# A gated mix of attention and a long convolution on one Trainium2 core: the convolution's tail taken in two halves of the channels

## The chip, the cores and the metric

One core of a Trainium2 chip (trn2) runs the whole computation in one launch. The metric is the device time of one execution in microseconds (us); lower is better.

## What is computed

With `x` of 2048 tokens by 512 channels in bf16, the result is `g*a + (1-g)*b`, where `g` is a sigmoid gate for each token. Cut to what matters, the reference is:

```python
x = A_x
g = sigmoid((x * gate_w).sum(-1, keepdims=True))
# a: 32 heads of 16 channels, 4 segments of 512 tokens, taken in order
for s in range(4):
    p = softmax(causal(q_s @ k_s.T * scale))
    o_s = gh * (phi(q_s) @ M) / (phi(q_s) @ z) + (1 - gh) * (p @ v_s)
    M, z = M + phi(k_s).T @ v_s, z + phi(k_s).sum()
a = concat(o) @ wo
# b: for each channel a kernel K of 2048 lags made of 128 complex exponentials,
# a causal convolution of x with K by FFT, and a skip term
K = einsum('dn,dnl,dn->dl', C, exp(dt*A*l), dt*B).real
b = irfft(rfft(pad(x)) * rfft(pad(K)))[:2048] + x * Dskip
return g * a + (1 - g) * b
```

## The kernel before

The program is recorded as a graph of operations (helpers `op`, `dma` and `evac`, L176 to L247) and replayed in an order that is written out as the string `ORDER` (L372): a list of the numbers of the operations, with a letter for those evictions that may run on either VectorE (`v`, called DVE) or ScalarE (`a`, called ACT). Each engine runs its share of that list strictly in the list's sequence, and so does the one DMA queue, which belongs to SyncE (SP). An operation waits on semaphores for what it reads and for the buffers that it takes. Almost every PE instruction of the program carries the line L646, every eviction L240 to L244 and every transfer L236, since helpers record them.

The work falls into these parts.

- *Powers* (`ssm_powers`, L741): ten repeated squares of a complex exponential for the two halves of the channels, 20 tiles of 2 KB in each partition (pool `pw`). DVE copies and negates parts of each tile (L761, L763).
- *Attention* (`project`, `scores`, `seg_state`, `ophase`): 4 segments by 4 groups of 8 heads. A group has five score tiles. For each, PE writes scores to four of the eight PSUM banks, ACT takes the exponential of 128x2048 elements (L1021, 80 of them), and PE multiplies by the values (`pv`). All else shares the other four banks.
- *Tables* (`tables`, L1090): the kernel K is built for 128 channels at a time, c = 0 to 3. DVE makes two tables of powers, F (20 entries) and G (32 entries), by complex products in three instructions each (L1118, L1121, L1125), in a layout with two channels side by side (inner runs of 2 elements). PE then multiplies them with many small matmuls of 20 columns (`lag`), and four transfers put the result in `KTT`. There is one buffer for F and one for G.
- *First level of the transform* (`x_level1`, L800): 32 matmuls of 512 columns over `x`, evicted and written to a scratch in DRAM, `scr_Z`.
- *Tail of the convolution* (`tail`, L1173): 16 steps t over the frequencies, each for all 512 channels. Step t loads 256 KB of `scr_Z` (Zx) and 448 KB of constants (CT, the tensor `c_DN`). `X`: two matmuls with the matrix M2, two evictions, and two transfers that swap the tile's halves of partitions. `K`: for each of two frequencies, five matmuls of 512 columns over `KTT` and an eviction. `Y`: a product on DVE (L1220). `V`: two matmuls each and an eviction. One transfer then scatters 256 KB to 8 partitions of `V2`.
- *Final* (end of `tail`): for each of 16 row blocks, `fin` adds the attention's output projection and the skip term, `fir` adds two matmuls over `V2`, and a scaled eviction and a transfer write the result. Six of the `fin` may run before the last V.

The tail's buffers (pools of phase 2, from `a = T0`) lie over F, G, the powers and the tables' scratch. A tile of phase 2 waits until the tiles of phase 1 that lay there are done with, so no step of the tail can load before the last table is used.

Of the kernel before, what the change touches and what calls it, by code (L numbers as in the profile page):

```python
# [11 lines left out]
H = 32  # L12
# [100 lines left out]
class Sched:  # L113
# [120 lines left out]
    def dma(self, out, in_, nbytes, r=(), w=(), pw=(), key=None, slow=False, q="SP"):  # L234
        kw = {"allow_slow_non_contiguous": True} if slow else {}
        return self.op(q, ("D", nbytes), lambda e: e.dma_start(out(), in_(), **kw), r=r, w=w, pw=pw, key=key, isdma=True)  # L236

# [118 lines left out]
def c_pe(mode, *ns):  # L356
    return ("P", mode, ns)


LQ = "SP"  # L360
NPT = 5
GA, TA0 = 2.6, 10.0
TT0, TT = 8.0, 26.0
XL0, XLS = 20.0, 20.0
TK0, TDK = 120.0, 7.0
NOPEN = 6
PW, PWS = (1.0, 8.0), 0.6
# [5 lines left out]
192 53 0 204 8 394 9 14 12 13 54 10 56 11 55a 15 22 28 57v 16 3 26 23a 1 24 17 27v 25a 1234 29 30 202 376 32 31 33 4  # L373
34 252 203a 18 35 36 44 2 199 253a 37 39 20 38 40 249 19 41 200a 42 21 43 201 211 172 5 173 7 218 219 45 6 47 207 48
46 49 52 58 209 174 50 175 61a 51 220 67v 68 69 66 176 59 60 72 212v 70 239 62 64 63 240 71 188 82 84 65 205 85a 83 78
241 86 87 189 190 191 193 76 227 194 97a 228 77 210a 98 99 94 208v 195 229 73v 213 74 75 95 96 106 108 235 90 206a 236
107 109v 118 221 120 237 119 133v 134 135 110 111 121a 196 79v 222 130 80 122 223 123 88 131 132 91a 234 144 224 238
89 102 242 177 243 178 142 225 100 179 226 230 143 145a 157v 154 156 103a 158 155 159 197 101 250a 114 112 1240 146
115a 147 113 124 126 104 127a 105 125 136 138 116 214 117 137 139a 150 180 148 166a 149 160 162 181 163a 161 92 169a
93 198 128 1002a 170 1003a 171 1008 1004a 129 251 1005a 215 261 1006a 1007 1241a 1010 262 1011 151a 1012 182 1009 1242  # L380
263 1016 183 184 1235 185 186 187 1017 1018 1236a 1022 265 1243a 1023 266 1244 1024 1237 267 1013 295 1014 1015 216
164 165 1238a 81 140 270 141 296a 271 231 1239 232 233 217 272 1025 292 377 1026 293a 278 378a 279 1027 379 280 1255
264 268 1038 269 273 274 380a 282 275 276 283 294 244 245 254 246 284 1245 152 153 1019 247 1020 1021 1028 248a 306
1029 255 307 1246a 1030 256 1247 257 308 277 1034 281 258 1037 1248a 311 1249 259 312 260 1039 1250 313 1252 1035 336
1276 1036 1251a 302 1253a 303 333 337a 167 1254 168 304 1031 1266 1268 1032 285 286 287 288 334a 289 319 1033 1267a
320 290 321 305 1040 309 291v 310 314 1256 1041 1258 1042 1269a 323 1043 1257a 324 1044 1270 1259a 1045 297 318 335
325 322 315 1260 316 1046 317 1047 1048 1049 298 345 1050v 346 299 1051 347 300 1052 1053 1054 301 1060v 1061v 1062v
1063a 1064v 349 1055a 1068 350 1069 1056 1070 1261 1074 351 1263 1057 326 1075 327 1058 1076 1078 1059 328 329 330
1262a 354 1080 1264a 355 1081 331 1265 356 386 1082 348 1083 352 353 332a 362 1084 387a 363 389 364 1271 1085 357 390a
358 366 359 1272a 367 360 393 391 1273 388 1092 338 591 368 1277 392 1093 1274a 408 339 1094 1275 409 1278a 1279 410  # L390
397 340 341 1280v 1065 1281 1066 1067 412 398a 1071 413 1072 342 1073 414 399 1077 343 344 443 1079 1086 400a 361 1087
425 444a 426 365 1088 427 401 1089 395 1090 402a 1091 429 396a 430 445 1098 411 431 1099 446 1100 1101 1282 1102 369
370 1103 447a 415 609 371 417 1283a 372 450 418 373 448 1095 374 419 1284 381 416 449 382 375v 493 1096 1285a 462 383
384 1286 463 494a 385 424 495 420 464 1097 403 1292 428 432 421 433 422 434 404 435 458 436 1293a 459 423 1104 405 460
1105 406 1106 1107 1109 1108v 1110 475 476 1111 477 1112 461 1113v 407 1118v 1114 1124 1294 1119v 1120v 1121a 1287
1115 1122v 479 1295a 1126 480 1127 1116 1288a 1128 1289 1117 1132 481 465 1133 496 1296 1134 1297 1138 466 1139 1290a
467 497a 468 1291 1140 592 498 500 1141 594 469 806 499 1142 593a 523 524 1143 470 525 1298 1123 1125 1129 1299a 1130
515 1131 595a 516 471 472 473 1300 1135 517 1136 541 1137 1144 1145 1301a 451 1146 542a 1302 1303 452 1147 1305 1304a
1148 1306a 474 506 1149 1307 507 543 1308 453 508 478 454 1310 1156 455 1157 482 1158 483 456 1309a 527 484 1311a 485
528 486 457 1312 437 529 1150 544 1313 438 439 545a 440 510 1314a 511 548 1151 546 441 512 487 1315 547 442v 488 509  # L400
489 1316a 490 565 566 1317 1152 513 567 514 491 522 1153 526 501 530 492a 531 1154 556 502 557 601 558 532 533 534 518
1155 549 602a 560 1159 550 561 1160 604 1161 562 503 504 1162 603 551 1163 552 1164 519 520 605a 1165 521 573 1166a
608 574 606 1167 575 1168 607 1169 1170 505 1171v 553 1176v 1172 1177a 1182 1178a 623 1194 1173 1179a 554 624 1180a
535 1174 555 625 1184 559 1175 536 563 537 564 538 568 711 569 570 571 644 712a 1181 645 1183 713 715 539 1185 658
1186 646 714 1190 1191 610 1192 1196 596 540a 627 1197 659a 628 611a 1198 572 576 629 1187 616 1188 1189 612 1199 617a
577 613a 578 1200 614 579 1201 661 615a 1212 632 662a 633 626 634 1193 630 1195 631 807 1202 580 1203 581 824 808a 640
1204 641 660 635 1208 642 639 636 1211 690 691 1213 643 692 1209 647 648 1210 677 678 597 582 598 599 583 600 809 637
638 679 584 1205 618 666 1206 810a 673 1207 674 1214 675 708 1215 1216 1217 1218 619 1338 1219 694 667 709v 695 1357
620 1220 1358 696 621 668 1221 1319 669 1222 710 1223 1320 649 650 1225 651 1339 1226 1224a 1227 1228 738 1318 1229a
739 676 1230 740 680 1231 681 585 1232 622 586 587 1233 670 663 588 682 683 671 589 672 684 664 759 590v 665 756 760v  # L410
721 757a 722 652 758 723 689 693 763 653 697 654 698 655 685 761 686 775 687 776 688 699 1351 700 777 701 762 1332
1352v 780 1333a 781 724 782 1327 702 1328v 771 703 772 704 997 705 773 706 998 999 742 1000 707a 1001 743 774 744 716
816 778 817v 779 783 717 730 784 731 785 786 656 718 732 719 819 818 657v 720 820v 764 725 821 823 737 726 765 822 741
766 727 745 767 746 954 747 748 749 768 955v 837 769 728 838 729 770 733 800 734 735 825 736 801 802 788 839 826a 789
803 871 790 956 750 872v 831 875 873 751 752 792 832a 793 753 911 874 794 754 912v 862 755v 811 833 913 812 827 813
834 815 829 828v 787 814 830v 842 791 835 843 795 863 864 796 957 797 798 799 865 958a 804 854 844 959 905 805v 855
849 906 836 907 840 908 841 845 960 850 846 847 868 848 851 856 914 869v 1321 870 915a 1323 852 897 1322v 1395 1324a
1359 898 853 918 1325 1360v 1361 857 1326 1362v 858 1340 1342 1414 1341v 1343a 1363 1397 859 885 1398a 860 1364 1399
861 886 1344 1329 866 1345 1334 1330 1376 1370 867v 1331a 1433 887 1400a 1335 1371v 916 1401 1346 1336a 1353 1402 1372
1337 1354 1347a 1378 899 1377 1380 1355a 876 1566 1379v 1381a 1365 877 1348 1382 917 1383 1373 1366v 1349 1374v 1435  # L420
1453 1350a 1437 979 1367 1436a 1384 1356 1438v 980 1471 878 1439 1368 1385v 879 1440 1369v 1416 1418 1396 1417a 880
981 1389 1375 1386 1419a 1528 881 961 1420 1465 1390v 1421 1391 1387 1466a 882 893 1388a 1392 894 883 1415 1393v 884
888 1473 889 1475 1394 1474v 1403 1452 1476v 1408 895 1477 1404a 890 891 1478 1405 923 1409a 948 924 1410 1406 1460
1407v 949 950 1422 1461a 951 925 1411 1423a 1454 1472 1412v 1456 1455a 892 919 1490 1424 1457a 896 1413 920 1425 1458
900 1426v 901 1427 1459 902 903 904 928 921 1428a 909 929 1429 922 926 910v 1479 1467 1430 1480a 930 1468 1434 1431a
1492 1481 936 1469a 1432 1494 1493v 937 927 1484 1509 1495v 1462 1496 931 935 932 1497 1485a 1463 938 966 933 1491
1464a 1486 1441 967 934 1470 1487 1442v 1482 1488v 1511 1529 1483a 940 968 1513 1512a 1489 1530 941 1514v 939 1547
# [9 lines left out]
1629 1661 1642a 1643 1662 1659 1663a 1660v 1664  # L437
"""


def v2_row(t):
    return 64 * (t >> 3) + 32 * ((t >> 2) & 1) + (t & 3)

# [903 lines left out]
```

## Time and profile before

Three timed runs gave 379.22, 384.55 and 379.0 us; the median is 379.22. The profiled execution took 382.91 us, of which the span from the first to the last instruction is 381.1.

| | PE | DVE | ACT | DMA |
|---|---|---|---|---|
| busy, us | 298.8 | 275.0 | 275.1 | |
| share of the span | 78% | 72% | 72% | 31% of 16 engines |
| instructions or packets | 4268 matmuls | 627 | 322 | 25755, 36.07 MB |

Busy time is the time in which at least one instruction of the engine was under way. A matmul's end is modelled, so a busy PE need not be a PE at its best rate. The clock granted to PE was 0.87 of its full rate on the mean. The shares are averages over stages that differ much, so the stages are read one by one in the prediction.

### The profile page before, as it was taken

Reading aid. Unit: us, or ns where it says so; the run is one execution under the profiler, and the core shown is the slowest. Engines: PE = TensorE matmul, PEld = TensorE weight load, DVE = VectorE, ACT = ScalarE, POOL = GpSimd, SP = SyncE. Lnnn points to the kernel's source line nnn. Section 1 sums busy time; section 2 is a strip of 40 time slices with the busy share of each in tenths; the row PEclk is TensorE's granted clock in tenths of the full one; section 3 lists DMA queues with packets and bytes.
Section 4 is the critical chain, followed back from the end, with each engine's and each line's share of the span. In section 5 each row is a group of like instructions: output and inputs, shape, how many; then the busy total and the mean of one; then the engine's idle time right before and its main releaser. Section 6 shows DMA issues by size and latency. Waiting matters only on the chain.

```text
span 381.1 us, 9878 instructions
## 1 busy us (share of the span) xinstructions
PE 298.8 (78%) x4268; PEld 170.4 (45%) x4268; DVE 275.0 (72%) x627; ACT 275.1 (72%) x322; POOL 3.2 (1%) x9
## 2 busy tenths in 40 slices
PE   3856167877696768879955899999969888788994
PEld 3314024455353534556532657655323433334551
DVE  0699999996998499978996352989768687644011
ACT  4599999788995589797965485789947786544242
POOL 1000000000000000000000000000000000000000
PEclk9965559689997586999968696999989999999998
DMA  7900002121200061101005500002797587663113
GB/s 180 321 15 1 3 28 84 64 104 49 84 29 29 3 184 58 57 3 21 2 2 156 204 3 2 2 2 56 233 248 210 172 245 210 187 174 110 34 75 146
DMA packets 25755, 36.07 MB, mean 95 GB/s; under 512 B 9200, under 2 KB 13808, under 8 KB 25584
## 3 DMA queue, kind: packets, MB, share of 16 engines
q1 hardware_dynamic: 25712, 35.45, 31.0%
q8 instruction: 33, 0.54, 0.6%
q14 instruction: 10, 0.08, 0.1%
HBM read 20.10 MB, written 6.29 MB: 69 GB/s over the span
## 4 chain that ended last, share of the span: by engine, by line
DVE 40%; PE 34%; DMA 14%; ACT 5%; issue 5%; SPq 2%; ACTq 0%
PE psum L646 33%; DVE sb L1118 8%; DVE sb L1125 8%; DVE sb L1121 7%; DMA sb<-c_DN 5%; DMA sb<-sb 5%; DMA sb<-scr_Z 3%; DVE sb L241 3%; ACT sb L1021 2%; DVE sb L996 2%; SPq L236 2%; DVE sb L753 1%; DMA sb<-in_B_C_im_dram 1%; DVE sb L752 1%; DVE sb L763 1%
## 5 line engine op out<-in xcount | busy, mean ns | idle before, releaser
L646 PE MATMUL psum<-sb 128*128 128x17 bf16 (+12 forms) x4132 | 287.2, 239 | 68.9 <-ACT sb L1021 21.6
L646 PEld LDWEIGHTS psum<-sb 128*128 128x128 bf16 (+3 forms) x4132 | 159.9, 100 | 193.9 <-issue 46.8
L1021 ACT ACTIVATE sb<-psum 128x2048 bf16<-128x2048 f32 x80 | 150.3, 1879 | 26.9 <-PE psum L646 26.4
L240 ACT ACTIVATE sb<-psum 128x512 bf16<-128x512 f32 (+2 forms) x143 | 85.0, 623 | 49.5 <-PE psum L646 41.4
L241 DVE CAST sb<-psum 128x512 bf16<-128x512 f32 (+1 forms) x66 | 43.7, 675 | 34.1 <-PE psum L646 29.4
L1118 DVE TENSOR_TENSOR sb<-sb 128x512 bf16<-128x512 bf16 (+3 forms) x52 | 35.8, 690 | 0.8
L1125 DVE TENSOR_TENSOR sb<-sb 128x512 bf16<-128x512 bf16 (+3 forms) x52 | 34.7, 669 | 1.5
L1121 DVE TENSOR_TENSOR sb<-sb 128x512 bf16<-128x512 bf16 (+3 forms) x52 | 35.5, 685 | 0.1
L1220 DVE TENSOR_TENSOR sb<-sb 128x1024 bf16<-128x1024 bf16 x32 | 21.7, 687 | 7.7 <-ACT sb L240 4.7
L244 DVE TENSOR_SCALAR sb<-psum,sb 128x512 bf16<-128x512 f32 x5 | 3.8, 751 | 21.4 <-PE psum L646 21.4
L243 ACT ACTIVATE sb<-psum,sb 128x512 bf16<-128x512 f32 x11 | 7.6, 687 | 14.8 <-PE psum L646 14.8
L996 DVE TENSOR_TENSOR sb<-psum,sb 128x256 bf16<-128x256 f32 x32 | 13.4, 423 | 0.9
L1033 DVE TENSOR_TENSOR sb<-sb 128x1024 bf16<-128x1024 bf16 (+1 forms) x20 | 11.5, 573 | 0.0
L751 ACT ACTIVATE sb<-sb 128x512 f32<-128x512 f32 x18 | 11.0, 626 | 0.1
L684 PE MATMUL psum<-sb 128*128 128x128 bf16 x64 | 5.8, 254 | 6.1 <-DMA sb<-c_ident 4.7
L993 DVE RECIPROCAL sb<-psum 128x16 f32<-128x16 f32 x32 | 8.0, 250 | 1.2 <-PE psum L646 1.1
L943 DVE TENSOR_SCALAR sb<-sb 128x512 bf16<-128x512 bf16 x16 | 5.6, 349 | 4.4 <-ACT sb L240 4.4
L759 ACT ACTIVATE sb<-sb 128x512 bf16<-128x512 f32 x14 | 8.7, 620 | 0.0
L952 ACT ACTIVATE sb<-sb 128x512 bf16<-128x512 bf16 x12 | 7.6, 634 | 1.3 <-PE psum L646 1.0
L1075 DVE TENSOR_TENSOR sb<-psum,sb 128x512 bf16<-128x512 f32 x12 | 8.3, 689 | 0.3
L1071 DVE SCALAR_TENSOR_TENSOR sb<-psum,sb 128x32 f32<-128x32 f32 x12 | 2.2, 184 | 8.3 <-PE psum L646 8.3
L684 PEld LDWEIGHTS psum<-sb 128*128 128x128 bf16 x64 | 4.8, 115 | 7.1 <-DMA sb<-c_ident 4.7
(65 smaller groups left out, 116.3 us busy)
## 6 DMA issues: line engine op xcount, KB each, us to landing
sb<-c_DN SPq DMA_DIRECT2D x16, 448.0 KB, 5.5
sb<-in_A_x_dram SPq DMA_DIRECT2D x8, 512.0 KB, 3.7
scr_Z<-sb SPq DMA_DIRECT2D x16, 256.0 KB, 2.0
sb<-scr_Z SPq DMA_DIRECT2D x16, 256.0 KB, 5.1
sb<-sb SPq DMA_DIRECT2D x32, 128.0 KB, 5.1
sb<-sb SPq DMA_DIRECT2D x16, 256.0 KB
out_dram<-sb SPq DMA_DIRECT2D x8, 256.0 KB, 2.1
sb<-c_M SPq DMA_DIRECT2D x1, 1024.0 KB, 6.4
```

The costliest lines, as they stand in the source:

```text
L240: fa = lambda e: e.activation(dst(), src(), ACT.Copy)
L241: fd = lambda e: e.tensor_copy(dst(), src())
L646: mm = lambda e, o_, l, r_, st, sp, **kw: e.matmul(o_, lhsT=l, rhs=r_, start=st, stop=sp, skip_group_check=True, **kw)
L684: i = e.transpose(ap(P, t2 * 512 + k * 128, n=128), ap(xks, (2 * hb + t2) * 512 + k * 128, n=128), ap(ident, n=128))
L751: op("ACT", ("As", 512), lambda e, sq=sq, Z=Z: e.activation(ap(sq, n=512), ap(Z, n=512), ACT.Square), r=[Z], w=[sq], key=PW[h] + PWS * k)
L996: op("DVE", ("V1", 256), lambda e: e.tensor_tensor(ap(o1, gi * 16, [[128, 4], [32, 4], [1, 16]]), ap(T, dims=[[68, 4], [17, 4], [1, 16]]), ...
L1021: o = op("ACT", ("Ax", 2048), lambda e, P=P, pT=pT: e.activation(ap(pT, n=2048), ap(P, n=2048), ACT.Exp, scale=0.25), r=[P], w=[pT])
L1033: op("DVE", ("V2", 128 * nb), lambda e, pT=pT, dims=dims: e.tensor_tensor(ap(pT, dims=dims + [[1, 128]]), ap(pT, dims=dims + [[1, 128]]), ...
L1118: op("DVE", ("V2", 256 * n), lambda e: e.tensor_tensor(run(tile, ne, dst, 1), run(tile, ne, src, sstep), ap(pw, cl * 512, [[2, 128], [0, n ...
L1121: op("DVE", ("V2", 256 * n), lambda e: e.tensor_tensor(run(t2, n, 0, 1), run(tile, ne, src, sstep), ap(pw, cl * 512 + 256, [[2, 128], [0, ...
L1125: op("DVE", ("V2", 256 * n), lambda e: e.tensor_tensor(D_(), D_(), ap(t2, n * 128, [[-n * 128, 2], [2 * n, 64], [1, 2 * n]]), ALU.add), r= ...
L1220: op("DVE", ("V2", 1024), lambda e, Y=Y, XAB=XAB, K3=K3, pi=pi: e.tensor_tensor(ap(Y, dims=[[512, 2], [1, 512]]), ap(XAB, pi * 512, [[1024 ...
```

## The change

The tail is made twice, once for each half of the channels (256 each), as soon as that half's tables exist. The first half takes its buffers in the memory of the first half's powers (`pwa`), which tables 0 and 1 alone read. Its V goes to a scratch in DRAM (`scr_V`) and is loaded to `V2` later in two transfers of 1 MB; the second half's V goes to `V2` directly, over 16 partitions. Every matmul of X, K and V has 256 columns where it had 512, and there are twice as many. The constants, now with M2's part in them (`c_DNM`, 512 KB a step), are loaded in each half. `x_level1` is split in the same way.

Beside this, the tables' layout has four channels side by side; F has two buffers and the scratch `t2` one; G is written in an order that puts its upper half first; a `lag` operation is half as long, so that others can stand between; the copies in the power tiles from the third power on are transfers instead of DVE instructions (`DUPK`); the parameters are loaded through ACT's queue; `wo` is loaded late; and `ORDER` is a new list. In the list the tables stand earlier against the attention than before. SP's queue has 261 transfers, before 151, and ACT's has 7.

Cut to its core:

```diff
-    pwP = mkpool("pw", 2048, 20)
+    pwPs = [mkpool("pwa", 2048, 10)]
-    FPs = [mkpool("F0", 10240, 1)]
+    FPs = [mkpool("F0", 10240, 2)]
...
-    t2P = mkpool("t2", 4096, 2)
+    t2P = mkpool("t2", 4096, 1)
...
+    a = PW0
+    for n, (nct, nzx, nk, ny, nv, nx) in enumerate(((2, 2, 2, 1, 2, 2), (3, 3, 2, 2, 2, 2))):
+        if n == 1:
+            a = T0
+            V2P = mkpool("V2", 32768, 1, 2)
+        tlP.append({"CT": mkpool("CT%d" % n, 4096, nct, 2), "Zx": mkpool("Zx%d" % n, 1024, nzx, 2), ...
...
-            run = lambda T, E, e0, st: ap(T, 2 * e0, [[2 * E, 128], [2 * st, n], [1, 2]])
+            run = lambda T, E, e0, st: ap(T, 4 * e0, [[4 * E, 64], [4 * st, n], [1, 4]])
...
-            for sl0 in range(0, 16, 4):
+            for sl0 in range(0, 16, 2):
...
-    def tail(k0, dk):
+    def tail(h, k0, dk):
         for t in range(16):
+            pl = tlP[1 if h == 1 and t % 2 == 0 else 0]
...
+            def f(e, PK=PK, CT=CT):
+                for pi in range(2):
                     for kt in range(5):
-                        i = mm(e, ap(PK, n=512), ap(CT, kt * 256 + pi * 128, n=128), ap(KTT, kt * 32, [[160, 16], [1, 32]]), kt == 0, kt == 4)
+                        i = mm(e, ap(PK, pi * 256, n=256), ap(CT, kt * 256 + pi * 128, n=128), ap(KTT, 1280 * h + kt * 32, [[160, 8], [1, 32]]), ...
...
-            S.dma(lambda t=t: ap(V2, 0, [[1024, 16], [1, 1024]], p0=v2_row(t), np_=8, pstep=4),
+            if h == 0:
+                S.dma(lambda kt=kt, tl=tl: bass.AP(Vd, tl * 8192 + kt * 4096, [[65536, 16], [512, 8], [1, 512]]), lambda V=V: ap(V, n=512), ...
+            else:
+                S.dma(lambda kt=kt, tl=tl: ap(V2, 8192 + kt * 4096, [[512, 8], [1, 512]], p0=tl, np_=16, pstep=8), lambda V=V: ap(V, n=512), ...
...
+            for kt in range(2):
+                def f2(e, Ps=Ps, g2=g2, kt=kt):
+                    for pi in range(2):
+                        for bl in range(2):
+                            i = mm(e, ap(Ps[bl], n=512), ap(G2T, (2 * kt + pi) * 128, n=128, p0=64 * bl, np_=64), ...
+                                   tile_position=(64 * bl, 0))
```

## The prediction, made before the changed kernel ran

> **What bounds the kernel now.** I read the busy time by stage first, with the stages cut at the exponentials: the first starts at 22.4 us, the 37th at 163.3, the last at 329.7. The columns are the stretch, its length, each engine's busy us, the granted clock, the DMA share and GB/s.
>
> ```profile
> 22.40:163.30 140.90, 100.50 (x1733) 59.01 (x1734) 126.58 (x304) 121.04 (x147) 0.66 (x1) 0.76 0.16 53
> 163.30:180.00 16.70, 13.76 (x414) 9.23 (x413) 13.30 (x40) 14.30 (x18) 0.00 (x0) 1.00 0.06 13
> 180.00:204.00 24.00, 19.12 (x257) 10.99 (x253) 23.38 (x40) 19.20 (x20) 0.66 (x1) 0.79 0.01 1
> 204.00:261.00 57.00, 51.42 (x972) 35.57 (x971) 33.39 (x92) 38.35 (x34) 0.00 (x0) 0.88 0.19 62
> 261.00:330.00 69.00, 58.79 (x556) 26.26 (x553) 52.56 (x103) 50.44 (x58) 0.00 (x0) 0.98 0.73 205
> 330.00:381.00 51.00, 41.59 (x274) 21.96 (x272) 15.58 (x26) 18.92 (x29) 0.00 (x0) 0.97 0.38 115
> ```
>
> Busy order is PE, PEld, DVE, ACT. To 204 us DVE is the bound (90% to 163, 97% from 180). From 204 to 261 the tables are over and the tail can't start, since its buffers lie over theirs: DVE falls to 59%, DMA to 62 GB/s, and PE sets the pace. From 261 the tail runs beside the last segment and DMA rises to 73%. The chain of waits shows what that costs:
>
> ```profile
> 206.21 3.51 issue
> ...
> 268.07 3.28 PE psum L646 x14
> ...
> 272.10 6.99 DMA sb<-c_DN
> 279.23 7.92 PE psum L646 x51
> ...
> 288.60 7.26 DMA sb<-scr_Z
> ...
> 298.24 4.39 DMA sb<-sb
> ```
>
> Transfers of 5 to 7 us stand in series with PE. The first line is another loss: inside `lag3` PE stood for 3.5 us with no wait shown (lag0 to lag2 lost 1.3, 2.3 and 1.5), and DVE's next eviction stood behind it.
>
> **Work.** The order is written out, so what stands ahead of each exponential can be counted, each instruction at the mean time it occupies its engine, PE's at its start-to-start time when packed at full clock (a K of five 512-column matmuls 1.11 us, a V 0.43, a group of score matmuls 0.33, a projection 0.86). This gives, in us (before | after):
>
> - ahead of the 37th exponential: ACT 132 | 143, DVE 137 | 151, PE 85 | 92
> - from there to the last one: ACT 121 | 111, DVE 123 | 107, PE 124 | 120
> - after it: ACT 18 | 15, DVE 15 | 17, PE 40 | 38
>
> The totals agree (about 270, 275, 250). So nothing large is removed; the change can only pack the same work better. At the last exponential the changed order has 6 X, 6 K and 8 V of 32 left; before it had 2, 8 and 10.
>
> **The parts.**
>
> *Ahead of the 37th exponential.* Before had done 150.1 us of DVE work at 180 us (10.25 to the first exponential, then rows one and two), so at the same density the changed kernel gets there at 180. From this come off: (a) DVE's waits at a `lag`, 1.0, 2.1, 4.2 and 2.0 us for the first three. A second F buffer gives DVE 16 of a chunk's 47 entries to go on with, and the halved `lag` operations let PE do other work between. I take 6 of the 9.3 us; bounds 0 and 9.3. (b) The layout of the tables.
>
> ```profile
> L1125 DVE TENSOR_TENSOR sb<-sb 128x512 bf16<-128x512 bf16 x16 | 6.8, 426 | 0.5
> L1125 DVE TENSOR_TENSOR sb<-sb 128x256 bf16<-128x256 bf16 x12 | 4.9, 416 | 0.3
> L1118 DVE TENSOR_TENSOR sb<-sb 128x256 bf16<-128x256 bf16 x12 | 4.8, 406 | 0.1
> ```
>
> 256 elements in inner runs of 2 (416 ns) cost as much as 512 in runs of 4 (426). The adds of 512 and of 1024 elements (692 ns) differ by 266 ns, so 256 elements in runs of 4 should take 426 - 133 = 293 ns; say 300, for the 36 instructions 3.8 us less; some 45 ns of excess on the 56 products of 512 and 1024 elements would be 2.5 more. I take 4; bounds 0 and 6. The Trainium skill speaks against this term: by "VectorE: DVE Perf Modes", section "Side-by-side: where the cycles go for N=2048 bf16", a bf16 tensor_tensor takes two elements a cycle whenever its step is 1, so 256 elements would take (128+150)/0.96 = 290 ns in either layout. The measured 406 says that short strided runs lose that rate; by the rule the term would be 0. (c) Sixteen copies of 226 ns leave DVE for transfers (3.6 us, already in the 151); these stand on SP's queue at a time when DMA is 16% busy. (d) Parameters through ACT's queue: the last one landed at 9.3 us, issued behind others at about 0.5 us each on SP; but ACT and DVE do 3 us more before the first exponential. 0; bounds -1.5 and +3. Stage: 180 - 6 - 4 = 170; bounds 163 and 182.
>
> *To the last exponential.* No filler of one kind is left; projections, states, 43 exponentials and 23 steps of the tail are mixed, and PE is the largest, 120 us. Its packed work over time was 45 of 57 us (79%) from 204 to 261, of which 90% in the last 21 us, and 53 of 69 (78%) from 261 to 330. The first contains the stall of `lag3`, the second the transfers above. The changed kernel moves 25 MB here in about 142 us, 180 GB/s where it was 205, and a step's packets are short: 128 of 4 KB at 159 ns, 512 of 1 KB at 46 ns, 44 us over 16 engines, 2.7 us, where a step with twice the channels took 3.1. So its transfers should land in 2.5 to 5 us rather than 5 to 7. I take 85%: 120/0.85 = 142 us. Bounds: 78% (nothing won), 154; 92%, as in the best stretch, 131.
>
> Matmuls of 256 columns: 288 more matmuls and weight loads. Four such matmuls, each with its load, start 0.109 us apart at full clock (scores at 241.95 us), half of the 0.213 of 512 columns, so the load hides: 0 us. Upper bound by the rows' busy means, 2 x 190 - 272 = 108 ns a pair, 31 us over the run (these means hold half-clock stretches). The skill has the rule that would make this the deciding cost: "TensorE: Matmul & The Clock Gate", section "The mechanism", says a weight load overlaps running matmuls only where the row group differs, which here it does not; at P/1.2 that page prices a load of 128 columns at 107 ns, so 288 of them add 31 us and the kernel comes out slower. The starts 0.109 us apart disagree with it.
>
> *The end.* 51 us for 40 of PE's work before; 38 now, 49 us. `fir` becomes 32 pairs of 64-row matmuls in two row groups. Four score matmuls of 512 columns in four row groups take 0.33 us, so a pair should take about 0.25 and the sum 8 us, where it was 7; if they don't overlap, 14. The last V's store (256 KB over 8 partitions before, 128 KB over 16 now) lies behind two `fin` and three `fir` of the first 1 MB. Stage: 49; bounds 46 and 56.
>
> Sum: 170 + 142 + 49 = 361 us of span, plus the 1.8 us by which the profiled time (382.9) exceeds its span (381.1): 363. That execution lies 1% above the median of the runs, 379.2; on their scale the forecast is **360 us**. The bounds that can hold together, 163 + 131 + 46 and 175 + 154 + 53, give 338 to 380 on that scale.
>
> **Rivals.**
>
> *Same mix, no better packing (within 2%).* PE stays at 78% because the four shared PSUM banks and strict queues set it, not the transfers. For it: both stretches gave 78 to 79%, and segments 1 and 2, whose states hold a bank, now lie in the mix. Against it: 90% from 240 to 261 with those same banks. 170 + 154 + 51 + 1.8 = 377, 373 on the runs' scale.
>
> *The tail's transfers hold PE in twice as many places (slower).* PE's queue is strict: an X or V that waits for its load or swap holds the scores behind it, these ACT, these the eviction that frees the next buffer. The first half has two CT buffers and one Y; the chain load 5.5, swap 5.1, X, K, Y, V and evictions about 3 is 14 us, two buffers make 7 us a step. SP's queue is strict too: a V store or swap that waits holds the next CT's load. The stops of 0.9 us and more in the tail's 16 steps were 3.1, 1.3, 1.1, 1.4, 2.3 and 1.5 us, 0.7 a step, and after one the clock was 0.5 for 3.4 us (the row at 279.23). Thirty-two steps at 0.7 us more than I allow make 22 us and eat the gain; at 0.9 us more, 29 us, the kernel is slower by 2%, and at 1.3, 403 us. Against it: DMA is less loaded, and tail steps of the first half have attention on both sides.
>
> *The early half doesn't run early.* Its buffers wait for the last use of `pwa`. Were the 32 steps pushed behind the tables, 8 MB of constants more at 205 GB/s would add 39 us. But three of its CT loads stand ahead of the 37th exponential in the list, and `pwa` has no reader after table 1. Part of the slower chance.
>
> **Chances and range.** A measurement here can tell about 2% from no change: 371.6 and 386.8 us. Forecast with its spread 0.62, no better packing 0.20, slower 0.18. The range, 341 to 388, takes in the bounds and leaves out the worse part of the slower case.
>
> **What would show it.** Right: the 37th exponential near 170 us, DVE's waits on a `lag` under 4 us in sum, the 256-element table rows near 300 ns; from there PE busy above 90% at a clock near 1 with no stretch like 204 to 261; the last exponential near 312; landings of CT and swaps under 5 us; 256-column starts still 0.11 us apart. Wrong: chain pieces of DMA of 5 us and more between 170 and 310, PE waiting on `c_DNM` or the swap more than 11 us in sum, or a clock of 0.5 in that stretch.

## The result, and the profile after

The changed kernel takes 353.3 us (median of 4 runs, 351.8 to 356.5) against 381.9 us before on the same chip: ratio 0.929, 95% interval 0.916 to 0.941. On a second chip it took 351.6 us, ratio 0.926 (0.920 to 0.933), and the experiments are read against this one. Executions of one kernel lie up to 3% apart, so the ratios compare the faster group of runs of each kernel. The forecast was 360 us, 0.949 of the 379.2 us on its scale; the measured ratio is 0.929. The profiled execution took 352.7 us with a span of 350.9 us.

Busy time by stage after the change, the columns as before: the first exponential starts at 23.9 us, the 37th at 160.9, the last at 302.5.

```profile
0.00:23.90 23.90, 12.71 (x79) 7.47 (x81) 11.27 (x33) 15.52 (x25) 1.87 (x7) 1.00 0.74 186
23.90:160.90 137.00, 102.00 (x2048) 63.71 (x2060) 130.49 (x312) 127.23 (x166) 0.67 (x1) 0.84 0.27 80
160.90:204.00 43.10, 39.73 (x751) 28.37 (x755) 31.92 (x69) 35.58 (x36) 0.67 (x1) 0.97 0.50 154
204.00:261.00 57.00, 55.66 (x803) 40.87 (x809) 41.71 (x97) 42.22 (x41) 0.00 (x0) 0.96 0.48 154
261.00:302.50 41.50, 35.94 (x540) 25.50 (x539) 32.92 (x72) 34.97 (x33) 0.00 (x0) 1.00 0.77 231
302.50:350.90 48.40, 40.05 (x343) 25.40 (x348) 18.84 (x33) 15.68 (x24) 0.00 (x0) 0.97 0.50 152
```

The stretch from 204 to 261 us, where DVE had been 59% busy and DMA moved 62 GB/s, is full: PE 98%, DVE 73%, 154 GB/s. The last exponential comes 27 us sooner, and from the 37th on PE is 93% busy (131.3 of 141.6 us). Ahead of the 37th DVE is the bound as it was, 95%, and the last product of the tables comes at 175.5 us where it came at 203.6. The chain of waits has lost most of its long transfers:

```profile
248.09 4.31 DMA sb<-sb
...
279.42 4.13 DMA scr_V<-sb
287.20 6.75 DMA sb<-c_DNM
299.82 4.89 DMA sb<-sb
```

One piece of over 5 us is left between 170 and 310 us (before: 6.99, 7.26 and, at 304.91, 5.51). The chain's pieces with no wait shown are 1.5 us at most, where the stall in `lag3` had been 3.5. The table rows:

```profile
L1152 DVE TENSOR_TENSOR sb<-sb 128x512 bf16<-128x512 bf16 x16 | 6.8, 426 | 0.5
L1152 DVE TENSOR_TENSOR sb<-sb 128x256 bf16<-128x256 bf16 x12 | 3.5, 293 | 0.4
L1144 DVE TENSOR_TENSOR sb<-sb 128x256 bf16<-128x256 bf16 x12 | 3.5, 289 | 0.2 <-ACT sb L240 0.2
```

256 elements now take 289 ns in the first product (L1144) where they took 406; 512 stay at 426 in the addition, whose runs were of four elements or more already.

### The profile page after: what moved, and what is told of

It reads as the page before. It is cut to its first block, busy times and chain, and to the rows that moved or that the text cites. A ratio compares the mean times of both kernels' runs of the same rounds, so it can differ in the third digit from the quotient of the medians.

```text
span 350.9 us, 10652 instructions
## 1 busy us (share of the span) xinstructions
PE 286.1 (82%) x4555; PEld 191.3 (55%) x4588; DVE 267.1 (76%) x611; ACT 271.2 (77%) x322; POOL 3.2 (1%) x9
## 4 chain that ended last, share of the span: by engine, by line
PE 36%; DVE 31%; ACT 13%; DMA 11%; SPq 4%; issue 3%; ACTq 2%; DVEq 0%
PE psum L662 35%; DMA sb<-sb 6%; DVE sb L1152 6%; DVE sb L1144 6%; DVE sb L1147 5%; ACT sb L1047 5%; SPq L236 4%; ACT sb L240 4%; DMA sb<-c_DNM 3%; DVE sb L241 3%; ACTq L236 2%; DVE sb L1253 2%; DVE sb L770 1%; DVE sb L769 1%; DMA scr_V<-sb 1%
## 5 line engine op out<-in xcount | busy, mean ns | idle before, releaser
L662 PE MATMUL psum<-sb 128*128 128x17 bf16 (+12 forms) x4419 | 277.0, 230 | 52.1 <-ACT sb L1047 19.2
L662 PEld LDWEIGHTS psum<-sb 128*128 128x128 bf16 (+4 forms) x4452 | 181.9, 104 | 144.6 <-ACT sb L1047 29.1
L241 DVE CAST sb<-psum 128x512 bf16<-128x512 f32 (+1 forms) x69 | 46.2, 680 | 20.6 <-PE psum L662 20.1
L1152 DVE TENSOR_TENSOR sb<-sb 128x512 bf16<-128x512 bf16 (+3 forms) x52 | 33.3, 641 | 1.5
L1144 DVE TENSOR_TENSOR sb<-sb 128x512 bf16<-128x512 bf16 (+3 forms) x52 | 33.1, 637 | 0.8 <-ACT sb L240 0.2
L1147 DVE TENSOR_TENSOR sb<-sb 128x512 bf16<-128x512 bf16 (+3 forms) x52 | 33.0, 635 | 0.0
L244 DVE TENSOR_SCALAR sb<-psum,sb 128x512 bf16<-128x512 f32 x8 | 5.6, 747 | 14.8 <-PE psum L662 14.7
L243 ACT ACTIVATE sb<-psum,sb 128x512 bf16<-128x512 f32 x8 | 5.1, 686 | 13.7 <-PE psum L662 13.7
L768 ACT ACTIVATE sb<-sb 128x512 f32<-128x512 f32 x18 | 11.3, 633 | 0.1
L733 DVE TENSOR_TENSOR sb<-sb 128x256 f32<-128x256 bf16 x2 | 0.8, 423 | 10.4 <-ACT sb L240 10.4
L927 ACT ACTIVATE sb<-psum 128x512 bf16<-128x512 bf16 x12 | 7.3, 612 | 1.1 <-PE psum L924 1.1
L770 DVE SCALAR_TENSOR_TENSOR sb<-sb 128x256 f32<-128x256 f32 x18 | 7.6, 424 | 0.4
L715 PE MATMUL psum<-sb 128*128 128x128 bf16 x24 | 2.7, 280 | 6.2 <-DMA sb<-in_B_A_im_dram 6.2
```

Source lines behind the costliest of these rows:

```text
L241: fd = lambda e: e.tensor_copy(dst(), src())
L662: mm = lambda e, o_, l, r_, st, sp, **kw: e.matmul(o_, lhsT=l, rhs=r_, start=st, stop=sp, skip_group_check=True, **kw)
L768: op("ACT", ("As", 512), lambda e, sq=sq, Z=Z: e.activation(ap(sq, n=512), ap(Z, n=512), ACT.Square), r=[Z], w=[sq], key=PW[h] + PWS * k)
L1144: op("DVE", ("V2", 256 * n), lambda e: e.tensor_tensor(run(tile, ne, dst, 1), run(tile, ne, src, sstep), ap(pw, cl * 512, [[4, 64], [0, n] ...
L1147: op("DVE", ("V2", 256 * n), lambda e: e.tensor_tensor(run(t2, n, 0, 1), run(tile, ne, src, sstep), ap(pw, cl * 512 + 256, [[4, 64], [0, n ...
L1152: op("DVE", ("V2", 256 * n), lambda e: e.tensor_tensor(D_(), D_(), ap(t2, n * 128, [[-n * 128, 2], [4 * n, 32], [1, 4 * n]]), ALU.add), r= ...
```

## The experiments

Differences are told as the ratio to the kernel before on the same chip, less the changed kernel's 0.926, times 382 us. By the two intervals such a difference is uncertain by some 4 us either way. Where stage marks are given, the changed kernel's are those of its second chip: first exponential 23.8 us, 37th 162.5, last 302.4, span 350.0. The 37th lay at 160.9 in the first profile of the same kernel, so a shift of 1 or 2 us in it says little.

> The changed kernel as it is, beside the next three, so that small differences can be read against it on one chip. Its ratio to the kernel before was 0.929; every theory expects 0.92 to 0.94, about 353 us.

Measured: 351.6 us, ratio 0.926 (0.920 to 0.933).

**The layout, taken back and put in alone.**

```diff
-            run = lambda T, E, e0, st: ap(T, 4 * e0, [[4 * E, 64], [4 * st, n], [1, 4]])
+            run = lambda T, E, e0, st: ap(T, 2 * e0, [[2 * E, 128], [2 * st, n], [1, 2]])
...
```

> The changed kernel with the tables back in runs of two channels; the order is the same. Theory 1 (DVE is the bound of the table stage, and short runs cost it the double rate): the rows of 256 elements go from 290 to about 405-416 ns, those of 512 from 422 to 465, those of 1024 from 690 to 742. That is 36 x 0.12 + 32 x 0.045 + 24 x 0.05 = 6.9 us of DVE time ahead of the 37th exponential, which moves from 160.9 to 166-168 us, and the kernel takes 358-360 us. Rival (ACT, 127 of 137 us busy in that stage, or PE sets the pace): the rows grow by the same, but the kernel by 2 us at most, 353-355 us.

Measured: 356.2 us, 4.6 more than the run beside it on the same chip; ratio 0.936 (0.930 to 0.942). The rows of the two products go back:

```profile
L1144 DVE TENSOR_TENSOR sb<-sb 128x1024 bf16<-128x1024 bf16 x12 | 8.9, 745 | 0.3
L1144 DVE TENSOR_TENSOR sb<-sb 128x512 bf16<-128x512 bf16 x16 | 7.5, 467 | 0.2
L1144 DVE TENSOR_TENSOR sb<-sb 128x256 bf16<-128x256 bf16 x12 | 4.9, 412 | 0.1
```

The 37th exponential moves by 2.8 us to 165.4 and the last by 4.1. Two thirds of the 6.9 us of DVE time reach the end, about half by the ratios (3.7 us): theory 1, a little under its numbers. The other way round, the kernel before with the same edit reversed and nothing else:

> The kernel before with the tables in runs of four channels, and nothing else of the change. The changed kernel lost 4.6 us (355.8 against 350.0 of span, 356.2 against 351.6 median) when it got the runs of two back. Theory (the layout is worth its 6.9 us of DVE time wherever DVE is the bound, to 204 us here): 4 to 7 us less than before, a ratio of 0.982 to 0.99. Rival (in the kernel before DVE waits at a lag and for F anyway, so a shorter table only waits longer): within 2 us, a ratio over 0.995.

Measured: 377.4 us against 384.7, ratio 0.984 (0.977 to 0.990), some 6 us. The layout alone is worth its DVE time there; the rival, a ratio over 0.995, lies outside the interval.

**The F buffers and the lag in pieces.**

```diff
-    FPs = [mkpool("F0", 10240, 2)]
+    FPs = [mkpool("F0", 10240, 1)]
```

and in the order, what writes the next chunk's F stands behind the last `lag` piece of the chunk.

> The changed kernel with one F buffer: what writes the next chunk's F is held in the order until the chunk's lag has read the last one; the lag stays in pieces of 16 matmuls. Theory 2 (the second F buffer is what removed DVE's waits at a lag): 5 to 9 us of these waits come back and the 37th exponential moves to 165-169 us; the kernel takes 358-362 us. Rival (the short lag pieces removed them, the buffer only lets the order run ahead): waits under 2 us, the kernel 353-355 us.

Measured: 371.9 us, 20 more; ratio 0.978. The 37th exponential comes at 179.4, 17 us later; from there to the end it is 191 us where it was 188. Theory 2 has the side and not the size. DVE at the start of the third chunk's table, in the timeline (start, duration, engine, line; in brackets the idle time before and what ended it):

```profile
112.89 0.44 DVE L949 COPY sb<-psum 128x272 f32<-128x272 f32 x1 [0.34 <-PE psum L662]
113.37 0.44 DVE L952 TENSOR_TENSOR sb<-sb 128x272 bf16<-128x272 f32 x1
116.32 0.35 DVE L969 TENSOR_SCALAR sb<-sb 128x512 bf16<-128x512 bf16 x1 [2.50 <-ACT sb L240]
120.77 0.29 DVE L1144 TENSOR_TENSOR sb<-sb 128x256 bf16<-128x256 bf16 x1 [4.10 <-ACT sb L240]
```

DVE has run out of other work: it waits until the lag has read the old F (its last matmul starts at 118.7 us) and ACT, behind an exponential, has copied the new chunk's first powers (line 240). With such waits DVE is 85% busy from 24 to 180 us, with two buffers 94% (first row: one buffer; second: the changed kernel):

```profile
24.00:180.00 156.00, 106.42 (x2054) 67.26 (x2066) 132.39 (x312) 128.71 (x167) 0.67 (x1) 0.79 0.24 70
24.00:180.00 156.00, 119.20 (x2299) 75.78 (x2312) 147.02 (x340) 143.93 (x182) 0.67 (x1) 0.85 0.28 86
```

Next, the pieces alone: in the order the eight pieces of each half chunk stand in one run (1112 to 1119 are those of the second chunk's first half):

```diff
...
-342 1139 1140 1112 1141 1113 1114 343 1115 1116 1117 344 401
+342 1139 1140 1112 1113 1114 1115 1116 1117 1118 1119 1141 343 344 401
...
```

> The changed kernel with two F buffers, but the eight lag pieces of each half chunk put in one run of 128 matmuls. Theory (a run of 128 small matmuls stops PE's own sequencer, 1.3 to 3.5 us in each of the four chunks before; the pieces avoid it): PE's waits with no cause shown rise from 2.4 to 7-10 us, the lag's eviction waits come back with 3 to 6 us, the kernel takes 354-358 us. Rival (the pieces do nothing, the order around them hid the stops): within 1.5 us of the changed kernel, 350-353.

Measured: 362.3 us, ratio 0.941 (0.934 to 0.949), 5.6 us more; the 37th exponential at 166.8. PE's waits with no cause shown rise to 4.2 us in 3 stops up to 200 us, from 1.9 in 9, less than the theory's 7 to 10. DVE's waits come up one step on, ahead of line 1019 (a normalisation of the attention). The rows up to 182 us, the changed kernel's first:

```profile
DVE sb L1019 <- PE psum L662: 2.4, 2, 1.4
DVE sb L1019 <- PE psum L662: 5.3, 3, 3.3
```

By the ratio the loss has the size of the theory; its place is not the eviction of the lag, where DVE waits only 0.3 us. The stops grew by 2.3 us and this wait by 2.9; that the stops cause the loss is argued from this, not shown.

> One F buffer as in the run before, with the lag pieces packed, so that F comes free earlier. The run with one F and spread pieces took 371.9 us, 20 more than the changed kernel, all of it ahead of the 37th exponential. Theory A (those 20 us come from the long life of F under the spread pieces; pack them and what is left is the wait of 9 us that the kernel before had): 358-363 us. Theory B (one buffer costs this in any order, since tables of the next chunk can't begin while ACT and PE work on the last): 367-374 us.

Measured: 370.9 us, ratio 0.962 (0.954 to 0.969): 13 us more than the changed kernel, 6 less than one F with spread pieces, 8 more than two F with packed ones. By the ratio that is 365 us on the scale of the second chip, between the theories: some of the 20 us is the long life of F under spread pieces, but packed pieces leave DVE three waits of 3.2 to 4.3 us for ACT's copies, one ahead of each later table. The two edits lean on each other: packing the pieces costs 5.6 us with two buffers and gains 6 with one, so the pieces need the second buffer.

**The place of the first half.** Order only: the tail's steps begin behind the last `lag`, the first K (1324) at the 1025th place instead of the 807th.

```diff
...
-481 1190 1324 1229 1230 1191
...
+712a 631 1324 677 586 713
...
```

> The changed kernel with the steps of the tail, both halves, moved back in the order behind the lag of the last table (their own sequence is kept, spread evenly from there to their old last place); all else keeps its order, memory and layout. Theory 1 (most of the gain is that the first half fills the place where only PE had work, 204 to 261 us before): the tables end at the same 176 us or a little sooner, but the last exponential no longer comes at 302 with six steps left; 13 to 20 us of the 31 come back, 365-372 us. Rival (the gain is the table stage, which the second F buffer shortened; the tail may stand before or after): 352-357 us.

Measured: 398.1 us, ratio 1.031 (1.021 to 1.040): 40 us more, slower than the kernel before. From the 37th exponential to the last one (the profiled run, 401.6 us, is the longest of its four, 5 us above the median of the others):

```profile
159.00:337.90 178.90, 144.89 (x2080) 98.94 (x2077) 103.96 (x230) 113.81 (x110) 0.69 (x1) 0.89 0.46 139
```

The 37th exponential is 3.6 us sooner, the last one 35 us later; PE is 81% busy and DVE 58%, at a granted clock of 0.89 where the changed kernel has 0.96. The tables end at 172 us, so in this order a short table stage brings nothing by itself. Theory 1, and beyond its numbers: nothing else in the order was rearranged for the late tail, so we take 40 us as an upper bound on what the place is worth.

> The changed kernel with the 16 steps of the tail's first half left out (their loads, X, K, swap, Y, V and stores); the first half of V2 is loaded from the scratch of x in the same size, so the output lacks that half of the convolution. By packed PE time these steps are 16 x (1.11 + 0.22 + 0.43) = 28 us. Theory 1 (they fill time in which PE had nothing else): 10 to 18 us less, 334-342 us. Rival (PE is the bound from the 37th exponential on, and its steps cost what they take): 27 to 32 us less, 320-325 us.

```diff
+        drop = [o for o in S.ops if o.tag.split(".")[0] in ("Zx0", "CT0", "X0", "K0", "Y0", "V0")]
...
```

Measured: 347.0 us, ratio 0.903 (0.895 to 0.910), 9 us less than the changed kernel, for 28 us of PE work. Its four runs spread from 342.8 to 349.4 us; by the two fastest it would be 12 us less. The stage, and in the waits of that stretch (us in total, times, longest) what PE waits for most, then the same wait of the changed kernel:

```profile
158.70:292.10 133.40, 111.30 (x1873) 75.11 (x1870) 81.30 (x195) 103.81 (x94) 0.67 (x1) 0.92 0.31 96
```

```profile
PE psum L661 <- ACT sb L1046: 16.9, 25, 1.5
PE psum L662 <- ACT sb L1047: 0.7, 2, 0.5
```

PE does 21 us less and waits 16.9 us for exponentials, which with the steps was 0.7; the stage is 7.0 us shorter (133.4 for 140.4). So most of the first half lies in time that PE would have spent waiting for ACT: theory 1, with a price at or just under the low end of its 10 to 18 us.

**Is there room left beside it?** Ten matmuls more in each of the first half's K, on PE alone:

```diff
-                for pi in range(2):
+                for pi in [0, 1] * (2 - h):
                     for kt in range(5):
```

> The changed kernel with the ten matmuls of each K of the first half issued twice into the same bank (the second overwrites the first): 16 x 1.11 = 17.8 us of packed PE work more, in the same place. Leaving out all of the first half (28 us of PE work) gave back only 8 to 10 us. Theory A (the first half fills time that PE has left, and there is more of it): 5 to 9 us, 357-361. Theory B (as ordered, PE is full: 98% busy from 204 to 261 us, so what is added now costs what it takes): 14 to 19 us, 366-371.

Measured: ratio 0.954 (0.948 to 0.959), 10.5 us more by it. The stage, ahead of it that of the changed kernel:

```profile
162.00:302.40 140.40, 132.55 (x2094) 96.23 (x2106) 107.35 (x239) 113.25 (x110) 0.67 (x1) 0.96 0.56 178
```

```profile
161.00:316.20 155.20, 147.66 (x2228) 108.83 (x2241) 107.33 (x236) 113.66 (x109) 0.69 (x1) 0.96 0.53 161
```

PE 15.1 us more, the stage 14.8 longer: one for one, theory B in this stage; by the ratio of whole runs, 10.5 of 17.8 us, it lies between the two. Taking PE work out gained 9 to 12 of 28 us, putting some in cost 10.5 to 14.8 of 17.8. We read this as PE and the exponentials close to balance here. The added matmuls come with weight loads of their own. Counted in the trace, this stage has 140 of these 256-column matmuls more (375 for 235), 14.8/140 = 106 ns each, and their starts lie 0.112 us apart, as in these 24 from the same run:

```profile
208.63 2.84 PE L662 MATMUL psum<-sb 128*128 128x256 bf16 x24
```

By the rule of the Trainium skill weighed in the prediction ("TensorE: Matmul & The Clock Gate", section "The mechanism"), that a load overlaps running matmuls only where the row group differs, an estimated load of 107 ns would have come on top of each; the run disagrees. The same section also lets a load into a background weight buffer run ahead; whether that is what happens here no run shows. Then transfers, 8 MB read and written that nobody waits for:

```diff
+        S.dma(lambda t=t: bass.AP(Wd, t * 262144, [[2048, 128], [1, 2048]]), lambda t=t: hC[t], 524288, run=4096)
```

> The changed kernel with an added copy of 512 KB from the constants to scratch memory, behind each of the first half's 16 loads of constants on SP's queue: 8 MB read and 8 MB written more, with no one waiting for it. Rival of the prediction (the tail's transfers hold PE): landings of the constants and swaps grow, PE waits on them more than 11 us in sum, and the kernel is 15 to 40 us slower, 366-390. Theory (transfers have room beside PE in this stage, DMA busy 57%): 0 to 5 us, 351-357.

Measured: ratio 0.955 (0.948 to 0.961), 11 us more, between the two expectations. The stage:

```profile
162.00:315.70 153.70, 137.17 (x2092) 97.72 (x2103) 107.14 (x238) 113.22 (x109) 0.66 (x1) 0.93 0.66 208
```

Median landings of the whole run grow little (constants 4.1 to 4.2 us, swaps 2.6 to 3.1; stores to `scr_V` 3.3 to 5.0), yet the stage is 13.3 us longer, 0.8 a step. PE's waits in the stage on Y (line 1253, here 1254) and on the constants, the changed kernel's first:

```profile
PE psum L662 <- DVE sb L1253: 1.7, 2, 1.5
PE psum L662 <- DMA sb<-c_DNM: 0.9, 1, 0.9
PE psum L663 <- DVE sb L1254: 5.8, 6, 1.7
PE psum L663 <- DMA sb<-c_DNM: 3.6, 3, 2.0
```

These are 6.8 us more, and PE is busy 4.6 us longer with the same work, at a granted clock of 0.93 for 0.96. The theory of free room is wrong: from 178 GB/s on, more transfers on this queue cost time. PE's waits on constants and Y, 9.4 us, stay under the rival's 11, and the loss under its 15, so the rival's mechanism is there in small; the change stays on its good side. Whether the bytes cost this or the 16 more places in SP's strict queue, the run does not tell apart.

**A better version?** The parameters, seven transfers, on SP's queue again (`PQ = "SP"`):

> The changed kernel with the eleven parameter loads issued from SP's queue again instead of ACT's. In the changed kernel the last parameter landed at 16.9 us (before: 9.3), the first DVE work was at 10.4 us (6.6) and the first exponential at 23.9 us (22.4). Theory 3 (slow issue on ACT's queue starts the whole chain late): first exponential at 21-22.5 us, and the kernel 1.5 to 3 us shorter, 350-352 us. Rival (the head start is lost again at the first point where another engine has the longer work, or SP's queue delays the weights and x instead): 353 us, no change.

Measured: 350.5 us, ratio 0.923 (0.917 to 0.929); first exponential 23.0 us (theory 3: 21 to 22.5), 37th 159.7, span 348.7. The last parameter lands at 15.5 us (issued at 9.7, landed 5.8 later), so the queue was the smaller part of the delay. This is the lowest median of a kernel that computes the whole result, 1.1 us under the changed kernel on the same chip, and the difference is too small to tell. With the negations on POOL besides:

```diff
-                op("DVE", ("V4", 256), lambda e, pw=pw: e.tensor_scalar(
+                op("POOL" if k >= 2 else "DVE", ("V4", 256), lambda e, pw=pw: e.tensor_scalar(
```

> A candidate: the changed kernel with the parameter loads on SP, and the 16 later negations of power tiles (128x256, 223 ns each on DVE, 3.6 us in all) on POOL, which does nothing else then. Theory (DVE is the bound to the 37th exponential, 93% busy): that exponential and the end come 2 to 3.5 us sooner than with the parameters on SP alone (350.5 us), 347-348.5. Rival (POOL and DVE share their way to memory and POOL takes longer over each, so table products wait for the negated tile or get slower): 350-354 us, DVE's table rows longer by more than 5 ns.

Measured: 353.2 us, ratio 0.920 (0.915 to 0.924), by the ratio not told apart from the run before; the 37th exponential comes at 161.0, 1.3 us later, the span is 351.1. Groups of POOL and DVE, the last two rows those of the run before:

```profile
L778 POOL TENSOR_SCALAR sb<-sb 128x256 bf16<-128x256 bf16 x16 | 16.5, 1036 | 44.2 <-DVE sb L777 31.3 <-ACT sb L776 12.9
```

```profile
L770 DVE SCALAR_TENSOR_TENSOR sb<-sb 128x256 f32<-128x256 f32 x14 | 6.3, 450 | 0.4
L777 DVE CAST sb<-sb 128x512 bf16<-128x512 f32 x4 | 1.9, 478 | 0.0
L770 DVE SCALAR_TENSOR_TENSOR sb<-sb 128x256 f32<-128x256 f32 x14 | 5.9, 424 | 0.3
L777 DVE CAST sb<-sb 128x512 bf16<-128x512 f32 x4 | 1.7, 422 | 0.0
```

POOL takes 1036 ns for 223, and DVE's operations beside it grow (424 to 450, 422 to 478 ns). Of the 3.6 us taken off DVE nothing is left: up to the 37th exponential it is busy 142.2 us in both runs. No gain is seen, as the rival has it, though the mean of the table rows grew by 7 ns at most (one product of 512 elements by 24) and the two runs come from different chips.

## Why the prediction was right, point by point

*From the 37th exponential to the last one*, 142 us predicted, 141.6 measured: 120 us of packed PE work in it is the 85% that was assumed. The mechanism is right; that the 85%, chosen between 78 and 92, met the time within 1 us is luck, since the second profile of the same kernel gives 139.9. PE is 93% busy, constants land in 3.9 us and swaps in 2.7, within the 2.5 to 5 forecast. That transfers hardly hold PE is right of the change as it stands; with 8 MB more they began to. Two of the signs of being wrong came up in small: the one chain piece of 6.75 us, and a clock near 0.5 twice for 3.4 us (the last three columns are clock, DMA share and GB/s):

```profile
201.60:205.00 3.40, 3.18 (x18) 2.40 (x18) 1.42 (x4) 2.23 (x2) 0.00 (x0) 0.51 0.85 289
222.10:225.50 3.40, 3.40 (x20) 1.87 (x18) 1.93 (x4) 1.93 (x2) 0.00 (x0) 0.50 0.37 157
```

*256-column matmuls*, 0 us: right, starts 0.112 us apart and 106 ns each by K issued twice. *The end*, 49 us predicted, 48.4 measured; the 64 matmuls of `fir` take 7.4 us where 8 were allowed.

*Ahead of the 37th exponential*, 170 us predicted, 160.9 measured: the one stage that was mis-sized, and 9 of the 10 us by which the span came out under the forecast. (a) 6 us for DVE's waits at a lag: of the 9.3 us none is left ahead of this mark, so 9.3. The evictions of the lag, over the whole run (before, then after):

```profile
L241 DVE CAST sb<-psum 128x320 bf16<-128x320 f32 x4 | 2.0, 491 | 7.7 <-PE psum L646 7.7
L240 ACT ACTIVATE sb<-psum 128x320 bf16<-128x320 f32 x4 | 1.7, 432 | 4.3 <-PE psum L646 4.3
L241 DVE CAST sb<-psum 128x320 bf16<-128x320 f32 x2 | 1.0, 488 | 0.9 <-PE psum L662 0.9
L240 ACT ACTIVATE sb<-psum 128x320 bf16<-128x320 f32 x6 | 2.7, 448 | 0.1
```

The new order also gives ACT six of the eight where it had four; ACT's waits there fell too, so the waits did not just move. (b) 4 us for the layout, bounds 0 and 6: the rows gained 6.9, 4.2 of it at 256 elements (3.8 counted) and 2.7 at the products of 512 and 1024, which the prediction priced at 2.5 and mostly left out. Taken back it cost 4.6 us, put in alone it won 6. The 290 ns that the prediction worked out from the Trainium skill ("VectorE: DVE Perf Modes", section "Side-by-side: where the cycles go for N=2048 bf16") is what runs of four take (286 to 293), and not what runs of two take (398 to 415). (c) Nothing for the copies sent as transfers: no wait of DVE or PE on them is in the list. (d) 0 for the parameters, upper bound 3: the first exponential came 1.5 us later, but DVE had done 1.0 us more by then (11.27 for 10.25), so 0.5 of it was lost. That leaves 180 - 9.3 - 6.9 + 0.5 = 164. The other 3 us are in two places. DVE had 151 us in the list ahead of the 37th exponential, 144 with the new rows, but had done 141.8 when it started (11.3 + 130.5): some 2 us ran later. So "stands ahead in the list" is not "must be done"; in the kernel before the two agreed (137 listed, 136.8 done), which hid that. And DVE's idle time behind the first exponential fell from 17.7 us (to 180 us) to 6.5, 1.9 more than the waits at a lag. In DVE's own time the sum closes: 8.3 us less work than the 150.1 at 180 us, 11.2 less idle and 0.5 lost at the start give 161.0.

What the prediction undervalued is the second F buffer. It was priced by waits of DVE that could be seen, 9.3 us; with one buffer the changed order loses 13 to 20. We take the waits seen before to be what an order made for one buffer had left over; this is a reading of those runs, not a measurement.

*The rivals.* No better packing: wrong, 93% busy. The tail's transfers: PE waited 3.6 us on constants in the whole run, but the run with extra transfers shows that the price is near, 0.8 us a step for 0.5 MB more read and written. The early half not running early: its first Y runs at 154 us, as the list had it. The stated range began at 341 us, though the prediction says that it takes in the bounds, of which the lower was 338.

Open is how the 28 us divide between the F buffers and the early half. The undo runs give 4 to 6 us for the layout, 8 to 20 for the buffer (packed pieces, spread pieces), up to 40 for the place, far more than the sum, since each leaves an order made for the others. An order rearranged for each undo was not tried.

## What to carry to other kernels

Look for the stretch where one engine works and the rest wait for memory, and give the work behind the wait other memory: 28 us of PE work then cost 9 to 12. Do not price a second buffer by the waits that remain alone: the order may have been made to avoid the others. And work listed ahead of a mark need not be done by then: count what the engine had really done.

## What was not expected of the hardware

- The last of the parameters landed at 16.9 us from ACT's queue and, in the same order, at 15.5 from SP's, against 9.3 before. Slow issues stood on both queues (ACT's last three parameters 1.05 to 2.3 us, SP's last two 1.6 and 1.0), where before each took 0.4 to 0.5. What made them slow no run shows.
- A negation of 128x256 took 1036 ns on POOL and 223 on DVE, and groups of DVE's float32 operations beside it took 3% to 13% longer in the mean (420 to 432, 424 to 450, 422 to 478 ns), two operations 47% (420 to 618).
- Median landings of constants and swaps that grew by 0.1 and 0.5 us went with a stage of 140 us that was 13 us longer: with strict queues the median does not tell what a transfer costs.
